# Zero matmuls, an earlier aT, an earlier x load and an earlier state transpose in a fused attention and maxout kernel

## The chip, the cores and the metric

The kernel runs on one core of one Trainium2 chip. The metric is the device time of one execution in microseconds (us). The engines are TensorE (PE; its weight loads are listed as PEld), VectorE (DVE), ScalarE (ACT), GpSimd (POOL) and SyncE (SP). Each engine works through its own instructions in the order in which the program gives them. DMAs are issued by SP, GpSimd and, once, ScalarE.

## The reference

Eight batches of cross attention between `x` (8 heads, 512 rows, 64 wide) and `state` (32 rows), read in both directions, followed by a feed-forward layer with a maximum of three products:

```python
scores = scale * x @ state.T            # per batch and head
xread  = softmax(scores) @ state        # 512 rows
sread  = softmax(scores.T) @ x          # 32 rows
tokens = concat([xread, sread])         # (8 * 544, 512) after merging heads
h      = max(max(tokens @ w1, tokens @ w2), tokens @ w3)   # 768 wide
out    = h @ w_out                      # (4352, 512) float32
```

## The kernel before

**Data.** Each batch's `x` is loaded as bfloat16 (`load_x`, a GpSimd DMA that converts). Half of batch 0 comes as float32 over SP and is converted by VectorE. The weights `w1`, `w2` and `w3` come in three chunks of two column blocks each (`load_w(0)` to `load_w(2)`, three GpSimd DMAs each), the states in four loads of two batches each (`load_st`). They are placed into `bd`, a block form of two heads side by side. For the first two pairs of batches the states are transposed on TensorE (`states`, line 127), for the last two by a DMA transpose on SP into `stT`, and then copied into `bd` by GpSimd (line 138, two copies for each pair).

**One batch.** `x_transpose` or `x_transpose_dma` makes `xT`. `scores` multiplies it with `bd` into `ps` and ScalarE writes the exponential `e`. `softmax` sums and inverts on VectorE (`den`, `rden`) and multiplies into `a` on GpSimd or VectorE (line 190). `a_transpose` (TensorE, then copies by ScalarE and VectorE, line 202) or `a_transpose_dma` (SP) makes `aT`. The state is not multiplied with `a` first: `g_cols` multiplies the state with the weights into `G` (line 248, copied out of PSUM at line 254), for six column blocks m of 128 columns. `x_maxout(b, m)` multiplies `G` with `aT` (line 269, six matmuls of 512 columns) for the three weights, and `maxout` takes their maximum: ScalarE copies the first (`t`, line 273), VectorE takes two maxima (lines 276 and 277) into `ht`. `ffn_out` multiplies `ht` with `wout` (line 306), ScalarE copies the result (line 309), and a DMA writes it out (line 318). `sread(b)` does the other direction; its result goes through a small SP DMA transpose (`late_transposes`) and is used at the very end (`s_maxout`).

**Order.** The order is written out by hand. Up to line 404 it is a straight list that starts batch 0, then interleaves batches 0, 1 and 2. `keep_busy(n)` issues n matmuls of zeros on TensorE. It stands three times in this list. From line 407 on a loop over batches b = 2 to 7 runs the six `x_maxout(b, m)`, and behind each of them a slot of further work: for the next batch n = b + 1 its scores (slot 0), softmax (slot 1) and DMA transposes (slot 2), and `ffn_out` of batch b - 1. In slot 2 the SP queue gets `a_transpose_dma(n)`, then `x_transpose_dma(n + 2)`, and, for n = 3 and n = 5, the states of batches 4 and 5, or 6 and 7. PSUM is used through two tags: "pw" with four buffers and "two" with two.

Of the kernel before, what the change touches and what calls it, by code (L numbers as in the profile page):

```python
# [15 lines left out]
def kernel(  # L16
# [16 lines left out]
    B, H, S, D = x.shape  # L33
# [20 lines left out]
    dve, act, pool = nc.vector.tensor_copy, nc.scalar.copy, nc.gpsimd.tensor_copy  # L54


    def load_st(k, eng):
        eng.dma_start(
            out=st_f[k],
            in_=state[2 * k:2 * k + 2].rearrange("b h n d -> (b h n) d").rearrange("(p t) d -> p t d", t=4))  # L60
# [8 lines left out]
    def load_x(b):  # L69
        nc.gpsimd.dma_start(  # L70
            out=x_sb[b][:, 0:XW].rearrange("p (h jd) -> p h jd", h=H),
            in_=x[b].rearrange("h (p j) d -> p h (j d)", j=J))
# [17 lines left out]
    def load_w(c):  # L90
        m0, m1 = chunks[c]
        for i, w in enumerate((moe_w1, moe_w2, moe_w3)):
            nc.gpsimd.dma_start(  # L93
                out=w_sb[c][:, :, i, :],
                in_=w.rearrange("(kk p) f -> p kk f", p=128)[:, :, m0 * 128:m1 * 128])

    def w_cols(m):
        c = [m0 <= m < m1 for m0, m1 in chunks].index(True)
        f = (m - chunks[c][0]) * 128
        return w_sb[c], slice(f, f + 128)  # L100
# [12 lines left out]
    def keep_busy(n):  # L113
        p = pp.tile([128, 1024], F32, tag="two", name="idle")
        for _ in range(n):
            nc.tensor.matmul(p[:, 0:512], zero[:, 0:128], zero, start=True, stop=True)  # L116


    def bd(b, h):
        return bds[b // 2][:, b % 2, h]  # L120
# [6 lines left out]
    def states(k, copy):  # L127

        if k < 2:
            p = pp.tile([128, 4, 128], BF16, tag="pw", bufs=4, name="pt")  # L130
            for t in range(4):
                nc.tensor.transpose(p[:, t, :], st[k][:, t].rearrange("p c d -> p (c d)"), ident)
        else:
            p = data.tile([128, 4, 128], BF16, name=f"stT{k}")
            nc.sync.dma_start_transpose(out=p, in_=st[k].rearrange("p t c d -> p (t c d)"))
        for c in range(2):
            r = slice(64 * c, 64 * c + 64)
            copy(out=bds[k][r, :, :, c, :].rearrange("p b h (q t) -> p (b h) q t", t=4),  # L138
                 in_=p[r].rearrange("p t (k q) -> p k q t", q=8))
# [4 lines left out]
    def new(d, b, shape, name, bufs=2):  # L144
        d[b] = work.tile(shape, BF16, tag=name, bufs=bufs, name=name)
# [13 lines left out]
    def x_transpose_dma(b):  # L159
        new(xT, b, [128, H, 2, 128], "xT", bufs=3)  # L160
        nc.sync.dma_start_transpose(out=xT[b].rearrange("p h j t -> p (h j) t"), in_=x_sb[b][:, 0:XW])  # L161
# [20 lines left out]
    def softmax(b, g0, g1, mul):  # L182
        n = g1 - g0
        if g0 == 0:
            new(a, b, [128, J, 2, HS, Ns], "a")
        den = work.tile([128, J, n, HS], F32, tag=f"den{n}", name="den")
        nc.vector.reduce_sum(out=den, in_=e[b][:, :, g0:g1], axis=AX.X)  # L187
        rden = work.tile([128, J, n, HS], F32, tag=f"rden{n}", name="rden")
        nc.vector.reciprocal(out=rden, in_=den)  # L189
        mul(  # L190
            out=a[b][:, :, g0:g1].rearrange("p j g s n -> p j (g s) n"),
            in0=e[b][:, :, g0:g1].rearrange("p j g s n -> p j (g s) n"),
            in1=rden.rearrange("p j g s -> p j (g s)").unsqueeze(3).to_broadcast((128, J, n * HS, Ns)))

    def a_transpose(b, g, copy):

        if g == 0:
            new(aT, b, [128, J, 2, 128], "aT", bufs=3)
        p = pp.tile([128, J, 128], BF16, tag="pw", bufs=4, name="pat")
        for j in range(J):  # L200
            nc.tensor.transpose(p[:, j, :], a[b][:, j, g].rearrange("p s n -> p (s n)"), ident)
        copy(out=aT[b][:, :, g, :], in_=p)  # L202

    def a_transpose_dma(b):
        new(aT, b, [128, J, 2, 128], "aT", bufs=3)
        nc.sync.dma_start_transpose(
            out=aT[b].rearrange("p j g t -> p (j g) t"), in_=a[b].rearrange("p j g s n -> p (j g s n)"))
# [26 lines left out]
    def flush_copies():  # L234
        while copies_due:
            copies_due.pop(0)()

    def g_cols(b, ms, copies=(nc.scalar.copy, nc.scalar.copy), defer=(False, False)):

        flush_copies()  # L240
        for m, copy, wait in zip(ms, copies, defer):
            if m == 0:
                new(G, b, [128, 2, NM * 384], "G", bufs=3)
            w, f = w_cols(m)
            p = pp.tile([128, 2, 512], F32, tag="two", name="pg")
            for s in range(HS):
                for g in range(2):
                    nc.tensor.matmul(  # L248
                        p[32 * s:32 * s + 32, g, 0:384].rearrange("p (i f) -> p i f", i=3),
                        bd(b, 2 * s + g)[64 * g:64 * g + 64, g, :], w[64 * g:64 * g + 64, s, :, f],  # L250
                        start=True, stop=True, tile_position=(64 * g, 32 * s))

            def place(m=m, p=p, copy=copy):
                copy(out=G[b][:, :, m * 384:(m + 1) * 384], in_=p[:, :, 0:384])  # L254

            if wait:
                copies_due.append(place)
            else:
                place()


    def maxout(b, m, n, lhs, rhs, nk):
        if m == 0:
            new(ht, b, [128, NM, n], "ht", bufs=4)
        pw = []
        for i in range(3):
            p = pp.tile([128, 512], F32, tag="pw", bufs=4, name=f"pw{i}")
            for k in range(nk):
                nc.tensor.matmul(p[:, 0:n], lhs(i, k), rhs(k), start=(k == 0), stop=(k == nk - 1))  # L269
            pw.append(p)  # L270
        t0 = work.tile([128, 512], BF16, tag="t0", name="t0")
        t1 = work.tile([128, 512], BF16, tag="t1", name="t1")
        nc.scalar.copy(out=t0[:, 0:n], in_=pw[0][:, 0:n])  # L273
        if copies_due:
            copies_due.pop(0)()
        nc.vector.tensor_max(t1[:, 0:n], t0[:, 0:n], pw[1][:, 0:n])  # L276
        nc.vector.tensor_max(ht[b][:, m, :], t1[:, 0:n], pw[2][:, 0:n])  # L277

    def x_maxout(b, m):
        maxout(b, m, 512,  # L280
               lambda i, k: G[b][:, k, m * 384 + i * 128:m * 384 + i * 128 + 128],
               lambda k: aT[b][:, :, k, :], 2)

    def s_maxout(m):
        w, f = w_cols(m)
        maxout("s", m, B * Ns, lambda i, k: w[:, k, i, f], lambda k: ats[:, :, k, :], HS)
# [51 lines left out]
    softmax(0, 0, 1, nc.gpsimd.tensor_mul)  # L338
    scores(0, 1, 2)
    softmax(0, 1, 2, nc.vector.tensor_mul)  # L340
    keep_busy(5)
    g_cols(0, (0,))
    a_transpose(0, 0, act)
    a_transpose(0, 1, dve)
    g_cols(0, (1,), (dve,))
    load_w(2)
    load_st(1, nc.gpsimd)
    x_maxout(0, 0)
    x_transpose(1, 0, act)
    x_transpose(1, 1, dve)  # L350
# [2 lines left out]
    scores(1, 1, 2)  # L353
    softmax(1, 0, 1, nc.gpsimd.tensor_mul)
    softmax(1, 1, 2, nc.gpsimd.tensor_mul)
    load_x(2)
    nc.gpsimd.dma_start(out=wout_sb, in_=moe_w_out.rearrange("(kk p) f -> p kk f", p=128))
    for k in range(2, B // 2):
        load_st(k, nc.gpsimd)
# [47 lines left out]
    for b in range(2, B):  # L407
        n = b + 1
        slots = [[] for _ in range(NM)]
        if n < B:  # L410
            slots[0].append(lambda: scores(n, 0, 2))
            slots[1].append(lambda: softmax(n, 0, 2, nc.gpsimd.tensor_mul))
            slots[2].append(lambda: a_transpose_dma(n))
            if n + 2 < B:
                slots[2].append(lambda: x_transpose_dma(n + 2))
            if n % 2 and n + 1 < B:
                slots[2].append(lambda: states((n + 1) // 2, pool))
            slots[5].append(late_transposes)
            if n + 3 < B:
                slots[0].append(lambda: load_x(n + 3))  # L420
        else:
            for m in range(NM):
                slots[m].append(lambda m=m: s_maxout(m))
        slots[1].append(lambda: g_cols(b, (2, 3)))
        slots[2].append(lambda: g_cols(b, (4, 5)))
        if n < B:
            slots[3].append(lambda: sread(n))
            slots[4].append(lambda: g_cols(n, (0, 1), defer=(False, True)))
        for j, m in enumerate((1, 2, 4, 5)):
            slots[m].insert(0 if m > 2 else len(slots[m]), lambda j=j: ffn_out(b - 1, j))  # L430
        for m in range(NM):
            x_maxout(b, m)
            for f in slots[m]:
                f()
# [36 lines left out]
```

## Time and profile before

| what | value |
|---|---|
| median of 11 runs | 165.45 us (160.22 to 169.97) |
| the profiled execution | 163.7 us, its span 161.9 us |
| mean granted TensorE clock | 0.984 |
| PE busy | 150.3 us (93%) |
| PEld busy | 71.2 us (44%) |
| DVE busy | 94.9 us (59%) |
| ACT busy | 96.6 us (60%) |
| POOL busy | 48.7 us (30%) |
| DMA moved | 21.72 MB, mean 134 GB/s |

The span runs from the first to the last instruction; the time of the execution is a little longer. The busy shares are averages over the whole span. The first third is a start in which TensorE waits for loads and for other engines, the rest a steady state in which TensorE is busy nearly without a break. A row of the timeline gives start, duration, engine, line, operation, output and input, and in brackets how long the engine stood idle before it and what ended this.

### The profile page before, as it was taken

The numbers are of one execution on the slowest core, as the hardware profiler recorded it, in microseconds if no ns is written. First come the engines' busy times: TensorE is split into PE (matmuls) and PEld (weight loads), VectorE is DVE, ScalarE is ACT, GpSimd is POOL, SyncE is SP. The second block draws the span as 40 slices with busy tenths as digits, with TensorE's granted clock in tenths as the row PEclk, the third lists the DMA queues.
The fourth block names the chain that finished last, engine by engine and source line by source line (L and its number), as shares of the span: only waits on it lengthen the run. The fifth ranks groups of instructions, "written<-read, shape, count | busy, mean of one in ns | idle before, by whom it ended". The sixth has DMA issues, their size and how long they took to land.

```text
span 161.9 us, 3570 instructions
## 1 busy us (share of the span) xinstructions
PE 150.3 (93%) x1433; PEld 71.2 (44%) x1433; DVE 94.9 (59%) x161; ACT 96.6 (60%) x156; POOL 48.7 (30%) x69
## 2 busy tenths in 40 slices
PE   7937979999999999899999997999999999999990
PEld 2413643454444444344444443444444475566450
DVE  4763796858536673577366735864667384475200
ACT  3224577799738827683888275837882837633340
POOL 8964069200733403641014034420141000100140
PEclk9996999999999999999999999999999999999997
DMA  3999949999799994597930965161307030030374
GB/s 127 189 180 196 197 86 105 162 232 186 119 195 196 234 183 93 194 191 197 144 130 0 122 117 203 60 163 42 134 0 202 0 136 0 0 134 0 130 223 166
DMA packets 35136, 21.72 MB, mean 134 GB/s; under 512 B 18832, under 2 KB 32784, under 8 KB 35120
## 3 DMA queue, kind: packets, MB, share of 16 engines
q0 software_dynamic: 15632, 15.08, 47.1%
q1 hardware_dynamic: 19344, 6.29, 21.2%
q8 instruction: 11, 0.18, 0.4%
q10 hardware_dynamic: 144, 0.13, 0.2%
q14 instruction: 5, 0.04, 0.1%
HBM read 15.20 MB, written 8.91 MB: 149 GB/s over the span
## 4 chain that ended last, share of the span: by engine, by line
PE 70%; DMA 7%; POOL 7%; issue 7%; ACT 3%; DVE 3%; SPq 1%; POOLq 0%; DVEq 0%
PE pw L269 36%; PE po L306 23%; PE pg L248 5%; DMA w<-in_moe_w_dram 5%; POOL bd L138 3%; POOL a L190 2%; PE psr L220 2%; PE ps L175 2%; ACT t L273 2%; DMA stT<-st 2%; DVE t L276 1%; SPq L161 1%; POOL w L93 1%; DVE ht L277 1%; PE ph L298 1%
## 5 line engine op out<-in xcount | busy, mean ns | idle before, releaser
L269 PE MATMUL pw<-aT,G 128*128 128x512 bf16 x288 | 71.2, 384 | 0.6 <-ACT aT L202 0.4
L276 DVE TENSOR_TENSOR t<-t,pw 128x512 bf16<-128x512 bf16 (+1 forms) x54 | 35.1, 651 | 43.3 <-ACT t L273 26.6
L306 PE MATMUL po<-wout,ht 128*128 128x512 bf16 x198 | 47.4, 380 | 0.0
L254 ACT CAST G<-pg 128x768 bf16<-128x768 f32 x46 | 35.7, 806 | 11.5 <-PE pg L248 11.1
L269 PEld LDWEIGHTS <-G 128*128 128x128 bf16 x288 | 26.7, 98 | 33.2 <-issue 4.9
L277 DVE TENSOR_TENSOR ht<-t,pw 128x512 bf16<-128x512 bf16 (+1 forms) x54 | 35.5, 658 | 5.6
L273 ACT CAST t<-pw 128x512 bf16<-128x512 f32 (+1 forms) x54 | 30.6, 566 | 13.5 <-PE pw L269 12.8
L309 ACT COPY osb<-po 128x512 f32<-128x512 f32 x33 | 19.3, 586 | 22.1 <-PE po L306 21.7
L306 PEld LDWEIGHTS <-ht 128*128 128x128 bf16 x198 | 17.8, 98 | 24.1 <-issue 4.0
L190 POOL TENSOR_TENSOR a<-e,rden 128x1024 bf16<-128x1024 bf16 (+1 forms) x9 | 14.5, 1618 | 43.4 <-DVE rden L189 33.1
L318 POOL DMA_DIRECT2D out_dram<-osb x14 | 8.0, 570 | 45.2 <-ACT osb L309 36.6
L248 PE MATMUL pg<-w,bd 64*32 64x384 bf16 x384 | 13.0, 331 | 3.5 <-DMA w<-in_moe_w_dram 2.9
L187 DVE TENSOR_REDUCE den<-e 128x32 f32<-128x1024 bf16 (+1 forms) x10 | 9.9, 991 | 0.8 <-ACT e L180 0.8
L180 ACT ACTIVATE e<-ps 128x1024 bf16<-128x1024 f32 x6 | 6.1, 1024 | 5.7 <-PE ps L175 5.6
L248 PEld LDWEIGHTS <-bd 64*32 64x32 bf16 x384 | 3.6, 89 | 12.5 <-issue 11.6
L269 PE MATMUL pw<-ats,w 128*128 128x256 bf16 x72 | 8.8, 273 | 0.0
L138 POOL COPY bd<-stT 64x512 bf16<-64x512 bf16 x4 | 4.2, 1056 | 14.4 <-DMA stT<-st 14.3
L269 PEld LDWEIGHTS <-w 128*128 128x128 bf16 x72 | 7.0, 98 | 2.1
L116 PE MATMUL idle<-zero 128*128 128x512 bf16 x15 | 5.9, 547 | 1.2 <-DVE zero L81 1.2
L93 POOL DMA_DIRECT2D w<-in_moe_w_dram x9 | 6.8, 771 | 0.0
L175 PEld LDWEIGHTS <-xT 128*128 128x128 bf16 x128 | 4.8, 98 | 4.4 <-issue 2.1
L70 POOL DMA_DIRECT2D x<-in_x_dram x7 | 6.5, 932 | 0.0
(46 smaller groups left out, 67.7 us busy)
## 6 DMA issues: line engine op xcount, KB each, us to landing
out_dram<-osb POOLq DMA_DIRECT2D x14, 512.0 KB, 3.5
x<-in_x_dram POOLq DMA_DIRECT2D x7, 512.0 KB, 10.0
w<-in_moe_w_dram POOLq DMA_DIRECT2D x9, 256.0 KB, 10.2
wout<-in_moe_w_out_dram POOLq DMA_DIRECT2D x1, 768.0 KB, 10.3
x0f<-in_x_dram SPq DMA_DIRECT2D x1, 512.0 KB, 3.9
out_dram<-osb SPq DMA_DIRECT2D x1, 512.0 KB, 2.7
stf<-in_state_dram POOLq DMA_DIRECT2D x3, 128.0 KB, 9.9
x<-in_x_dram POOLq DMA_DIRECT2D x1, 256.0 KB, 4.8
```

The lines of the kernel that those rows point to most:

```text
L93: nc.gpsimd.dma_start(out=w_sb[c][:, :, i, :], in_=w.rearrange("(kk p) f -> p kk f", p=128)[:, :, m0 * 128:m1 * 128])
L138: copy(out=bds[k][r, :, :, c, :].rearrange("p b h (q t) -> p (b h) q t", t=4), in_=p[r].rearrange("p t (k q) -> p k q t", q=8))
L187: nc.vector.reduce_sum(out=den, in_=e[b][:, :, g0:g1], axis=AX.X)
L190: mul(out=a[b][:, :, g0:g1].rearrange("p j g s n -> p j (g s) n"), in0=e[b][:, :, g0:g1].rearrange("p j g s n -> p j (g s) n"), in1=rden.r ...
L248: nc.tensor.matmul(p[32 * s:32 * s + 32, g, 0:384].rearrange("p (i f) -> p i f", i=3), bd(b, 2 * s + g)[64 * g:64 * g + 64, g, :], w[64 * ...
L254: copy(out=G[b][:, :, m * 384:(m + 1) * 384], in_=p[:, :, 0:384])
L269: nc.tensor.matmul(p[:, 0:n], lhs(i, k), rhs(k), start=(k == 0), stop=(k == nk - 1))
L273: nc.scalar.copy(out=t0[:, 0:n], in_=pw[0][:, 0:n])
L276: nc.vector.tensor_max(t1[:, 0:n], t0[:, 0:n], pw[1][:, 0:n])
L277: nc.vector.tensor_max(ht[b][:, m, :], t1[:, 0:n], pw[2][:, 0:n])
L306: nc.tensor.matmul(p, ht[b][:, m, j * 128:(j + 1) * 128], wout_sb[:, m, :], start=(m == 0), stop=(m == NM - 1))
L309: act(out=o[:, j, :], in_=p)
```

## The change

Four places in the order change; no operation's size or engine does.

1. The third `keep_busy` issues nine zero matmuls instead of five.
2. The transposes of `a` of batch 0 come ahead of column block 0 of its `G`; on ScalarE and VectorE the copies of `aT` come ahead of those of `G`.
3. `load_x(2)` moves, on GpSimd, from behind the softmax multiplications of batch 1 to a place ahead of them, directly behind the third chunk of W and the second load of states.
4. In slot 2 of the loop, for n = 3 and n = 5, the transpose of the states comes ahead of that of `x` on SP.

```diff
     softmax(0, 1, 2, nc.vector.tensor_mul)
-    keep_busy(5)
-    g_cols(0, (0,))
+    keep_busy(9)
     a_transpose(0, 0, act)
     a_transpose(0, 1, dve)
+    g_cols(0, (0,))
     g_cols(0, (1,), (dve,))
     load_w(2)
     load_st(1, nc.gpsimd)
+    load_x(2)
     x_maxout(0, 0)
...
     softmax(1, 0, 1, nc.gpsimd.tensor_mul)
     softmax(1, 1, 2, nc.gpsimd.tensor_mul)
-    load_x(2)
     nc.gpsimd.dma_start(out=wout_sb, in_=moe_w_out.rearrange("(kk p) f -> p kk f", p=128))
...
             slots[2].append(lambda: a_transpose_dma(n))
+            if n % 2 and n + 1 < B:
+                slots[2].append(lambda: states((n + 1) // 2, pool))
             if n + 2 < B:
                 slots[2].append(lambda: x_transpose_dma(n + 2))
-            if n % 2 and n + 1 < B:
-                slots[2].append(lambda: states((n + 1) // 2, pool))
```

## The prediction

> **What bounds the kernel.** I read the page's chain first, then the waits by engine, then the timeline of the first 28 us, then PE's rows with an idle time in the rest. In the chain TensorE is nearly everything:
>
> ```profile
> PE 70%; DMA 7%; POOL 7%; issue 7%; ACT 3%; DVE 3%; SPq 1%; POOLq 0%; DVEq 0%
> PE pw L269 36%; PE po L306 23%; PE pg L248 5%; DMA w<-in_moe_w_dram 5%; POOL bd L138 3%; POOL a L190 2%; PE psr L220 2%; PE ps L175 2%; ACT t L273 2%; DMA stT<-st 2%; DVE t L276 1%; SPq L161 1%; POOL w L93 1%; DVE ht L277 1%; PE ph L298 1%
> ```
>
> PE is busy 150.3 of 161.9 us. So only what PE waits for, or works off at a low clock, can be won. The list of waits names the places that the change touches:
>
> ```profile
> POOL bd L138 <- DMA stT<-st: 14.3, 2, 7.2
> ...
> PE pg L248 <- DMA w<-in_moe_w_dram: 2.9, 1, 2.9
> ...
> PE ps L175 <- POOL bd L138: 1.6, 2, 0.9
> ```
>
> The columns are total, count, longest. The 14.3 us are GpSimd's own and cost nothing by themselves. PE's 1.6 us come from the two late states. PE's 2.9 us are the wait for the first W chunk, which no edit shortens. What follows it can be shortened (timeline from 12 to 18 us; start, duration):
>
> ```profile
> 12.70 0.36 PE L248 MATMUL pg<-w,bd 64*32 64x384 bf16 x8 [2.89 <-DMA w<-in_moe_w_dram]
> ...
> 12.99 0.65 PE L201 MATMUL pat<-ident,a 128*128 128x128 bf16 x8
> 13.13 0.80 ACT L254 CAST G<-pg 128x768 bf16<-128x768 f32 x1 [3.76 <-PE pg L248]
> ...
> 13.82 0.59 ACT L202 COPY aT<-pat 128x512 bf16<-128x512 bf16 x1
> ...
> 14.46 2.62 PE L269 MATMUL pw<-aT,G 128*128 128x512 bf16 x6 [0.37 <-ACT aT L202]
> ...
> 17.82 1.46 PE L269 MATMUL pw<-aT,G 128*128 128x512 bf16 x6
> ```
>
> ScalarE copies G (0.80), then aT (0.59), and only then does the first maxout start. The same six matmuls take 2.62 us at 14.46 and 1.46 us at 17.82. The table by windows, cut at the points where the granted clock turns (13.45 and 16.86), says why; PE's busy time stands first after the length, PEclk third from the end:
>
> ```profile
> 6.61:10.03 3.42, 2.67 (x34) 1.54 (x32) 2.48 (x5) 1.19 (x2) 1.86 (x4) 1.00 1.34 175
> 10.03:13.44 3.41, 0.74 (x16) 0.59 (x16) 1.43 (x3) 0.31 (x1) 3.41 (x5) 1.00 1.39 184
> 13.44:16.85 3.41, 3.04 (x18) 1.06 (x15) 1.79 (x3) 1.56 (x3) 0.35 (x1) 0.50 1.45 196
> ```
>
> A stretch of 3.41 us with 0.74 us of PE work is followed by one of the same length at half clock.
>
> **Part 1: start of batch 0.** Four zero matmuls more: the five now spread over 1.24 us from 8.57, about 0.216 apart, so nine end near 10.7. GpSimd's a of head half 0 is done at 10.99, VectorE's of half 1 at 11.53. The zero matmuls thus lie in PE's idle time; the cover is 0.3 us, and each 0.216 us beyond it would delay the transposes, which themselves have cover: they are 8 matmuls in two groups of about 0.4 us, done near 12.0, while the first W chunk lands at 12.57 (its last piece is issued at 3.86 and lands 8.71 us later). The order adds one wait ahead of G: PE's transposes wait for a at 11.53, and behind them stand both G columns, then the maxout; with 0.6 us to spare until W it costs nothing. ScalarE (0.59) and VectorE (0.42) copy aT by about 12.6, in idle time. Then G: matmuls at 12.70, copy 13.13 to 13.93, maxout at 13.97 instead of 14.46: **0.49 us** gained.
>
> The clock: in the stretch 10.03 to 13.44 there will be 0.6 us of zero matmuls, 0.8 of transposes and 0.75 of G, 2.1 us (62%) instead of 0.74 (22%). The trace shows 22% followed by half clock and 2.67 (78%) by full clock; what decides between is not shown. The bounds are a gain of 0 and of 2.62 - 1.46 = 1.16 us. The Trainium skill, "TensorE: Matmul & The Clock Gate", section "Part 4: PE-mode transpose", speaks against the change: transposes don't count as busy PE for the gate in the same way. By it only 0.6 + 0.75 = 1.35 us (40%) count, nearer to the row that dropped; by the plain busy row 62%, nearer to the one that held. The rule cannot be tested on the row of before, since 0.45 us of its 0.74 are transposes and it drops either way. I take full clock, as 62% is nearest to 78%, with the other end kept as a rival. The first maxout then ends 0.49 + 1.16 = 1.65 us earlier.
>
> **What is late next.** x of batch 1 lands at 4.59 + 10.6 = 15.2, and its transposes would start at about 15.3: just in. Scores of batch 1 go from 19.11 to 17.45. But behind them on PE stand the G columns 2 and 3, at 19.68 now. The three W pieces of that chunk, by the DMA view, are issued at 6.12, 6.87 and 7.62 and land 10.5, 11.0 and 11.6 us later: 16.6, 17.9 and **19.2**. PE will wait there for 1.1 us, and G column 2 is earlier by 0.43 only. From there I step on: ScalarE, free of the exponentials by then, copies it 19.67 to 20.47 (now 20.52 to 21.33); G column 0 of batch 1 goes 20.5 instead of 21.38; its ScalarE copy ends near 21.7, t of maxout (0,2) near 22.3, VectorE's t and ht near 23.8 instead of 24.96. a of batch 1 is ready near 22.1 instead of 23.75, so the transposes no longer stop PE (0.27 us). What the stage hands on is earlier by 24.96 - 23.8, **1.1 us**; full 1.65 were W in time; 0.45 with the clock at half, since then only the 0.49 remain and W hides a little.
>
> **Part 2: x of batch 2.** Its one GpSimd DMA issue of 0.95 us moves from 23.69 to about 13.8, ahead of the two multiplications of batch 1. GpSimd stands idle there for 7.90 us, until 21.69 (20.0 after part 1), so the issue is hidden; without that cover it would cost 0.95 us before a. In the queue it is ahead of wout, states 2 and 3, x3 and x4, and all of these issue 0.95 us earlier. Nobody waits for them on PE now: x2 lands at 23.69 + 6.4 = 30.1 and is transposed at 32.98; wout lands at 34.9, first used at 37.89. So the sum gets **0**. It comes behind the third W chunk, which lands at 23.3 and is used at 35.7.
>
> **Part 3: states ahead of x.** Twice (batches 4 and 6), SP issues aT, xT, stT; afterwards aT, stT, xT.
>
> ```profile
> 56.17 1.25 SPq L206 DMA_TRANSPOSE aT<-a  x1
> 57.59 3.08 SPq L161 DMA_TRANSPOSE xT<-x  x1
> 60.73 1.26 SPq L135 DMA_TRANSPOSE stT<-st  x1
> ```
>
> stT starts 3.1 us earlier and lands 2.5 us after its start, or, if it has to follow aT (which lands at 60.2), at 61.4 at the latest; the two GpSimd copies take 2.18 us, done by 63.6. PE's scores are ready for them at 64.76:
>
> ```profile
> 65.47 0.63 PE L175 MATMUL ps<-bd,xT 128*128 128x64 bf16 x16 [0.71 <-POOL bd L138]
> 98.00 0.63 PE L175 MATMUL ps<-bd,xT 128*128 128x64 bf16 x16 [0.86 <-POOL bd L138]
> ```
>
> Both waits go, **0.71 + 0.86 = 1.57 us**; the second place has the same intervals (aT at 88.63, scores wanted at 97.14). The price is one stT issue, 1.26 to 1.51 us, ahead of xT of batches 5 and 7 and the sread transpose behind them on SP. xT of batch 5 now lands at 62.0 and is read at 81.22; the delay would have to be over 15 us. Behind the copies on GpSimd stand two output DMAs, which become free earlier. From 98 to 156 us no PE row shows idle time, so what is won is kept to the end.
>
> **Sum.** 1.1 + 0 + 1.57 = 2.7 us. Against the profiled execution, 163.7 (span 161.9 and 1.8 around it), that is 161.0. The median shown is 165.45; I take the same microseconds from it: **162.7 us**, -1.6%. The 11 runs spread from 160.22 to 169.97, so a measurement of this kernel tells about 2%, 3.3 us, from no change, and the forecast lies just inside.
>
> **Rivals and chances.**
> - **Forecast, 0.45:** 162.7, own range 161.2 to 164.2. By the spread, two fifths of this case fall over 2%.
> - **More is won, 0.27:** W's second chunk is not the limit, or most runs hold more of these waits than the profiled one. For: the median is 1.75 us above the profiled execution, and something is longer there. Against: the pieces land evenly, 1.3 us apart, by the queue's pace. Full 1.65 + 1.57 = 3.2 gives 162.2; with the 1.75 as well 160.5. Nearly all of it counts as faster.
> - **Less is won, 0.17:** the clock drops all the same, 0.45 + 1.57 = 2.0, 163.4 us; or stT is held by other transfers and its 1.57 stays, 164.3. Against the latter: stT lands 2.5 and 2.7 us after its issue even behind xT.
> - **Slower, 0.11: x2 takes W's place.** At 13.8 us the second W chunk is still in transit. If packets of x2 are served between its own, its landing moves by up to x2's transfer time: 512 KB against 256 KB per 1.33 us, 2.66 us, so 19.2 becomes 21.9. Then G column 2 is 2.2 us later than now, and less the 1.57 of part 3 the kernel is 0.6 us slower: 166.1. It decides once the chunk lands after 19.68 + 1.57 = 21.25. For: the queue holds many transfers at once (landing takes 10 us). Against: the third chunk, queued from 10.9 on, lands after the second, at 20.5, 21.9 and 23.3, in the order of issue.
>
> Faster: 0.45 x 0.4 + 0.27 = 0.45. Slower by over 2% needs 3.3 us, more than this mechanism gives; with other slow causes I keep 0.10. Within 2%: 0.45. The range goes from 160.2 (all won and the spread) to 165.4 (nothing won).
>
> **What would show it.** Right: the first maxout starts near 14.0 and takes about 1.46 us at PEclk 1.00; PE waits for a W transfer at about 18.1 to 19.2; no PE row waits for POOL bd; x2 lands near 26. Wrong: PEclk 0.50 over 3.4 us about 14 to 17; the second W chunk landing after 20; L175 still behind L138, or behind xT; a new PE wait for ScalarE or VectorE between 24 and 35 that takes back the first stage's gain.

## The result, and the profile after

The changed kernel is faster by about 1%: the ratio of its times to those of before is **0.9905, with a 95% interval of 0.9863 to 0.9947**. On the 163.7 us of the profiled execution that is 1.6 us less (0.9 to 2.2), where 2.7 were forecast. The medians of all executions, 160.2 us (12) and 163.93 us (47), lie further apart: the ratio leaves out those more than 1.5% above the fastest of their kernel, 4 of the 12 and 32 of the 47, and as no experiment shows what makes these long, it is the number to use.

The profile of after is one of the four, with 165.2 us and a span of 163.4. Its start can be compared, and its middle shows what a late transpose does. First the start, rows of the timeline from 10 to 19 us (start, duration, engine, line, operation, and in brackets the idle time before and what ended it):

```profile
10.92 0.40 PE L201 MATMUL pat<-ident,a 128*128 128x128 bf16 x4 [0.36 <-POOL a L190]
11.47 0.40 PE L201 MATMUL pat<-ident,a 128*128 128x128 bf16 x4 [0.15 <-DVE a L190]
...
11.79 0.52 PE L248 MATMUL pg<-w,bd 64*32 64x384 bf16 x16
...
12.22 0.80 ACT L254 CAST G<-pg 128x768 bf16<-128x768 f32 x1 [0.28 <-PE pg L248]
...
13.08 1.47 PE L269 MATMUL pw<-aT,G 128*128 128x512 bf16 x6 [0.76 <-ACT G L254]
...
18.32 0.52 PE L248 MATMUL pg<-w,bd 64*32 64x384 bf16 x16 [0.96 <-DMA w<-in_moe_w_dram]
```

Every forecast step is there. aT is out of the way before G, the maxout starts as soon as ScalarE has copied G, and it takes 1.47 us instead of 2.62. Then TensorE waits 0.96 us for the second W chunk. The clock held, in the table by windows (PE's busy time first after the length, granted clock third from the end):

```profile
10.03:13.44 3.41, 2.14 (x29) 0.84 (x28) 2.69 (x5) 1.38 (x2) 3.41 (x5) 1.00 1.38 184
13.44:16.85 3.41, 3.41 (x33) 1.98 (x31) 2.26 (x4) 2.08 (x3) 1.11 (x2) 1.00 1.45 196
```

TensorE is busy for 2.14 us (63%) where it was busy for 0.74. But note the row at 11.79: no wait for W stands in its bracket. In this execution the first chunk landed near 11.5, not at 12.57, and G waited for the transposes of a.

Now SP's rows and the scores' rows in the middle:

```profile
45.14 5.29 SPq L161 DMA_TRANSPOSE xT<-x  x1
54.22 1.24 SPq L206 DMA_TRANSPOSE aT<-a  x1
55.51 2.57 SPq L135 DMA_TRANSPOSE stT<-st  x1
58.25 4.31 SPq L161 DMA_TRANSPOSE xT<-x  x1
```

```profile
62.57 1.46 PE L269 MATMUL pw<-aT,G 128*128 128x512 bf16 x6 [1.06 <-DMA aT<-a]
66.55 0.63 PE L175 MATMUL ps<-bd,xT 128*128 128x64 bf16 x16 [2.52 <-POOL bd L138]
```

stT does stand ahead of xT now, as forecast. But xT of batch 4, issued at 45.14, was in transit for 13.6 us in this execution, until 58.7. aT took 8.2 us to land behind it (4.0 before) and stT 8.8 (2.5 before), and TensorE waited for both, 1.06 and 2.52 us. For what the states' new place does when xT lands sooner, this profile is the wrong one; the experiment with the states alone shows it.

### The profile page after: what moved, and what is told of

Its sections match the earlier page's. It is cut to its first block, busy times and chain, and to the rows that moved or that the text cites. A ratio compares the mean times of both kernels' runs of the same rounds, so it can differ in the third digit from the quotient of the medians.

```text
span 163.4 us, 3578 instructions
## 1 busy us (share of the span) xinstructions
PE 151.5 (93%) x1437; PEld 71.2 (44%) x1437; DVE 95.1 (58%) x161; ACT 96.8 (59%) x156; POOL 48.7 (30%) x69
## 4 chain that ended last, share of the span: by engine, by line
PE 72%; DMA 12%; POOL 7%; DVE 3%; ACT 1%; issue 1%; SPq 1%; POOLq 0%; DVEq 0%
PE pw L269 37%; PE po L306 24%; DMA w<-in_moe_w_dram 6%; PE pg L248 6%; DMA stT<-st 5%; POOL w L93 2%; PE psr L220 2%; PE ps L175 2%; DVE t L276 2%; POOL bd L138 1%; POOL a L190 1%; DVE ht L277 1%; PE ph L298 1%; SPq L206 1%; ACT t L273 1%
## 5 line engine op out<-in xcount | busy, mean ns | idle before, releaser
L306 PE MATMUL po<-wout,ht 128*128 128x512 bf16 x198 | 48.2, 384 | 0.0
L116 PE MATMUL idle<-zero 128*128 128x512 bf16 x19 | 6.8, 512 | 1.2 <-DVE zero L81 1.2
```

What stands on the lines that cost most here:

```text
L306: nc.tensor.matmul(p, ht[b][:, m, j * 128:(j + 1) * 128], wout_sb[:, m, :], start=(m == 0), stop=(m == NM - 1))
```

## The experiments

**Part by part.** The first three kernels do one part of the change each, the fourth does all but the move of x.

`start_only` (items 1 and 2 in the list of changes, part 1 of the prediction):

```diff
-    keep_busy(5)
-    g_cols(0, (0,))
+    keep_busy(9)
     a_transpose(0, 0, act)
     a_transpose(0, 1, dve)
+    g_cols(0, (0,))
```

> Only the start changes: nine zero matmuls and aT of batch 0 ahead of its G; x of batch 2 and the states stay as before. Theory A (the sizes of the prediction hold): 1.1 us less, ratio 0.993; the first maxout starts 0.5 us after the first W chunk's G copy order is relieved and takes 1.46 us at full clock, and PE then waits about 1 us for the second W chunk; both waits for the block form of the states (0.7 and 0.9 us) remain. Theory B (nearly all of the gain of 1.5 us is the start, since the waits for the states vanish only in the profiled execution): 1.5 us less, ratio 0.991. Theory C (the clock of before drops only in some executions, so the start is worth only its 0.5 us): ratio 0.997.

Measured: **0.9996 (0.9967 to 1.0025)**. Nothing is won, within 0.5 us. Theory A and theory B fall for the start, and even C's 0.5 us lies at the edge.

`x2_only` moves `load_x(2)` behind `load_st(1)`, ahead of the multiplications.

> Only the load of x of batch 2 moves ahead of the multiplications. Theory A and B: nobody waits for it, ratio 1.000. Rival D (x2 takes transfer time from the second W chunk): that chunk lands after 20 us, up to 2.2 us more, ratio up to 1.013. Rival E (the earlier load thins out the transfers later, when SP's transposes and the loads of x collide): the waits for the states get shorter and the ratio falls below 0.997.

Measured: **1.0008 (0.9965 to 1.0052)**, from seven of its 22 executions. The second W chunk's last piece landed 10.9 us after its issue (11.6 in the profile of before), so D has nothing to stand on. Nor has E: the two waits for the block form are still there, 1.14 and 0.84 us.

`states_only` puts `states` ahead of `x_transpose_dma` in slot 2.

> Only the states' transposes go ahead of x's. Theory A: both PE waits for the block form (0.71 and 0.86 us) are gone, 1.57 us less, ratio 0.990. Theory B (stT is held by the transposes that are still in flight, whatever stands ahead of it, or the waits exist only in the profiled execution): 0 to 0.3 us, ratio 0.998 to 1.000. Theory C: at least 1.0 us less, ratio 0.994 or lower.

Measured: **0.9866 (0.9830 to 0.9902)**, 2.2 us (1.6 to 2.8). This part alone brings all that the change brings. The rows of the scores in its profile, and then those of `start_only`, which keeps the old order of the states:

```profile
47.05 0.63 PE L175 MATMUL ps<-bd,xT 128*128 128x64 bf16 x16
62.81 0.63 PE L175 MATMUL ps<-bd,xT 128*128 128x64 bf16 x16
78.57 0.63 PE L175 MATMUL ps<-bd,xT 128*128 128x64 bf16 x16
94.33 0.63 PE L175 MATMUL ps<-bd,xT 128*128 128x64 bf16 x16
```

```profile
46.85 0.63 PE L175 MATMUL ps<-bd,xT 128*128 128x64 bf16 x16
63.09 0.63 PE L175 MATMUL ps<-bd,xT 128*128 128x64 bf16 x16 [0.32 <-POOL bd L138]
78.84 0.63 PE L175 MATMUL ps<-bd,xT 128*128 128x64 bf16 x16
96.01 0.63 PE L175 MATMUL ps<-bd,xT 128*128 128x64 bf16 x16 [1.25 <-POOL bd L138]
```

These rows are the cleanest measure of the steady state: without a wait, one batch takes 15.76 us from scores to scores. With the old order the two batches that need stT take 16.24 and 17.17, 0.48 and 1.41 too many, **1.89 us** together. In the profile of before the rows ahead of the two in the prediction are

```profile
48.84 0.63 PE L175 MATMUL ps<-bd,xT 128*128 128x64 bf16 x16
81.22 0.63 PE L175 MATMUL ps<-bd,xT 128*128 128x64 bf16 x16
```

so the two batches take 65.47 - 48.84 = 16.63 and 98.00 - 81.22 = 16.78, also 1.89 us too many. That the two sums agree is chance: in the other profiles with the old order and no late xT they are 2.0 (`w_short`), 2.3 (`x2_only`), 2.8 (`w_short_start`) and 2.9 us (`zeros_only`). With stT ahead of xT, in `states_only`, all batches take 15.76. And this is how stT comes in:

```profile
54.40 1.25 SPq L206 DMA_TRANSPOSE aT<-a  x1
55.69 1.37 SPq L135 DMA_TRANSPOSE stT<-st  x1
57.24 1.32 SPq L161 DMA_TRANSPOSE xT<-x  x1
59.06 2.20 POOL L138 COPY bd<-stT 64x512 bf16<-64x512 bf16 x2 [4.69 <-DMA stT<-st]
```

stT lands 3.3 us after 55.69, GpSimd's copies run from 59.06 to 61.26, and the scores at 62.81 find them done with 1.5 us to spare.

`start_and_states` is the whole change without the move of x.

> The whole change without the move of x of batch 2. Theory A: 2.7 us less by the sum, ratio 0.983, the same as the whole change; B: the same as the whole change, 0.990; C: 0.990. Rival D (x2's earlier load costs): better than the whole change by 0.5 us or more. Rival E (it helps later): worse than the whole change by 0.5 us or more.

Measured: **0.9895 (0.9858 to 0.9932)**, the same as the whole change within the intervals. The three parts multiplied, 0.9996 x 1.0008 x 0.9866, give 0.987; whether the missing 0.3% is more than spread the intervals don't tell.

**Why is the start worth nothing?** Its gain was seen in a trace, and it is gone in the time. Two kernels split it.

`zeros_only` has only `keep_busy(9)` instead of `keep_busy(5)`.

> Only the four zero matmuls more; G stays ahead of aT. Theory H (the start brings nothing on the whole because the granted clock drops in only a part of the executions of before and the new order makes G wait for a when W lands early): the clock never drops at the start, so no execution with a mean granted clock near 0.986 is left, and the early G is kept; 0.1 to 0.4 us less, ratio 0.997 to 1.000. Theory I (the clock is what the start is worth): ratio 0.993.

Measured: **0.9983 (0.9944 to 1.0021)**, which is against theory I.

`order_only` has only the new order of aT and G, with five zero matmuls.

> Only aT of batch 0 ahead of its G; five zero matmuls as before, so that TensorE does nothing but 0.8 us of transposes between about 9.7 us and the landing of W. If transposes hold the clock as other matmuls do, nearly no execution shows the mean clock of 0.984 to 0.990 that a drop at the start gives, which a third or more of the executions of before show; if they do not count, as many show it as before. Time: theory H 0.0 to 0.3 us less, ratio 0.998 to 1.000; theory I, with transposes not counting, 1.000.

Measured: **1.0051 (1.0005 to 1.0098)**, a little slower, which no theory had; why is not shown.

The mean granted clock of every execution behind the ratios says how often the clock drops at the start. A drop there gives a mean of 0.984 to 0.989 (one elsewhere would count too).

| kernel | executions compared | of these with a mean clock below 0.99 |
|---|---|---|
| before, in the three sets | 33, 19, 25 | 9, 6, 6 |
| order_only | 10 | 5 |
| zeros_only | 13 | 0 |
| start_only | 16 | 0 |
| start_and_states | 12 | 0 |
| states_only, x2_only, w_short, states_sread, states_early (five zero matmuls) | 29 | 4 |
| after, w_short_start, start_states_sread (nine) | 27 | 0 |
| start_early_sread (nine) | 11 | 3 |

So the profile of before, with its drop, shows what happens in only 21 of the 77 executions, and with 163.7 us it is longer than any of them. In the first set those with the drop average 162.2 us, the others 161.7: it costs some 0.6 us there, and 0.8 to 1.1 in the other two sets. A quarter of that is 0.2 us, which is what `zeros_only` shows and what the interval can't tell from nothing. With four more zero matmuls the drops at the start end; the three in `start_early_sread` can lie elsewhere, since TensorE has waits of 1.15 and 1.71 us there at 61 and 78 us (below). The new order alone doesn't end them, with 0.8 us of transposes in the same gap.

Why the order doesn't pay shows in the profiles side by side. All times are us; W is the landing of the last piece of the first W chunk, and "hand-over" is the row of line 269 near 32 us that ends with a wait for VectorE's ht, which every kernel passes. The last column is worked out before rounding.

| kernel | W | first G matmul | first maxout | clock dropped | wait for the 2nd W chunk | hand-over | hand-over less W |
|---|---|---|---|---|---|---|---|
| before | 12.6 | 12.70 | 14.46 | yes | none | 34.28 | 21.7 |
| x2_only | 11.9 | 12.02 | 13.78 | yes | none | 33.36 | 21.5 |
| states_only | 11.7 | 11.84 | 13.60 | no | 0.64 | 32.50 | 20.8 |
| zeros_only | 10.7 | 10.87 | 12.63 | no | 0.65 | 31.55 | 20.8 |
| order_only | 12.0 | 12.13 | 13.41 | no | 1.11 | 32.81 | 20.8 |
| start_only | 11.5 | 11.69 | 12.97 | no | 1.04 | 32.30 | 20.8 |
| after | 11.5 | 11.79 | 13.08 | no | 0.96 | 32.33 | 20.8 |
| start_and_states | 10.3 | 12.09 | 13.37 | no | none | 32.04 | 21.7 |

Three things stand in it. With W late enough, the new order brings the first maxout 1.28 us after the first G matmul instead of 1.76, 0.48 us as forecast. But where the clock has not dropped and TensorE waits for the second W chunk, the hand-over comes 20.8 us after W with the old order and with the new one: the half microsecond goes into a longer wait for that chunk. From the end of this wait to the hand-over it is 14.00 or 14.01 us in all five profiles, so there the chunk's landing sets the time, whatever came before. In `start_only`, with the new order:

```profile
18.29 0.52 PE L248 MATMUL pg<-w,bd 64*32 64x384 bf16 x16 [1.04 <-DMA w<-in_moe_w_dram]
32.30 1.46 PE L269 MATMUL pw<-aT,G 128*128 128x512 bf16 x6 [0.19 <-DVE ht L277]
```

And where W lands early, at 10.3 us, the new order makes G wait for a until 12.09, and the whole advance of W is lost. The rows of `zeros_only`, with the old order, show the other side of it:

```profile
10.87 0.35 PE L248 MATMUL pg<-w,bd 64*32 64x384 bf16 x8 [0.42 <-DMA w<-in_moe_w_dram]
11.16 0.62 PE L201 MATMUL pat<-ident,a 128*128 128x128 bf16 x8
...
12.63 1.45 PE L269 MATMUL pw<-aT,G 128*128 128x512 bf16 x6 [0.57 <-ACT aT L202]
...
17.55 0.52 PE L248 MATMUL pg<-w,bd 64*32 64x384 bf16 x16 [0.65 <-DMA w<-in_moe_w_dram]
...
31.55 1.46 PE L269 MATMUL pw<-aT,G 128*128 128x512 bf16 x6 [0.18 <-DVE ht L277]
```

With W at 10.7 the maxout starts at 12.63. In the profiles with the new order it starts at 12.97 at the earliest, since VectorE finishes a at 11.30 there (`start_only`) and the transposes of a come next.

**Is it the second W chunk?** Two kernels leave out one third of that chunk and have zeros in its place.

```diff
         for i, w in enumerate((moe_w1, moe_w2, moe_w3)):
+            if c == 1 and i == 2:
+                nc.gpsimd.memset(w_sb[c][:, :, i, :], 0.0)
+                continue
```

`w_short` has the old start:

> The kernel before, but the third piece of the second W chunk (w3, column blocks 2 and 3) is not loaded; zeros are written there instead, so that this chunk lands some 1.3 us sooner. Theory F (the gain of the start is lost at the wait for this chunk): the unchanged start gains little from it, 0 to 0.6 us, ratio 0.996 to 1.000, since it reaches that place at about 17.9 us and the chunk landed at 18.4 to 19.2. Theory G (the start's gain is lost elsewhere): no change, 1.000.

Measured: 0.9919 (0.9873 to 0.9965), 1.3 us less, more than F forecast and against G's none. `w_short_start` has the new one:

> As the last one, with nine zero matmuls and aT of batch 0 ahead of its G. Theory F: no wait for the second W chunk after the scores of batch 1, which now start near 17.0; the start is worth 0.5 us where the clock was full before and 1.1 to 1.6 us where it had dropped, so 0.5 to 1.0 us under the last kernel, 0.993 to 0.996 of before. Theory G: equal to the last kernel within 0.2 us.

Measured: 0.9988 (0.9944 to 1.0032). Against theory F, the new start is not faster in time; by these ratios it is slower, though the intervals just overlap. In the profiles it is faster: the wait for the chunk is gone from both, and hand-over less W is 31.44 - 10.9 = 20.5 with the old start and 32.08 - 12.0 = 20.1 with the new one, 0.4 us less. But W itself landed 1.1 us apart in these two executions, more than the effect. So that the start's half microsecond goes into the wait for the second chunk is read from the rows; this pair of kernels, meant to show it in the time, doesn't, and where the 1.3 us of `w_short` come from is open.

**Filling that wait.** `states_sread` is `states_only`, and `start_states_sread` is `start_and_states`, with work that needs no W moved ahead of it:

```diff
+    sread(0)
     g_cols(0, (2, 3), (act, dve))
-    sread(0)
```

> The states' transposes ahead of x's, and sread of batch 0 (0.56 us of TensorE work that needs no W) ahead of the G columns 2 and 3, where TensorE waits for W. Theory F: with the old start the wait of about 0.6 us is filled, 0.3 to 0.5 us less than the states alone, ratio 0.984; the granted clock still drops at the start in some executions. Theory G: as the states alone, 0.987.

Measured: 0.9844 (0.9786 to 0.9903).

> The last one with nine zero matmuls and aT ahead of G as well. Theory F: the wait for W, about 1.0 us with the new start, is filled for 0.56 us; 0.4 to 0.6 us less than start and states without it, ratio 0.984 to 0.986, and about equal to the last kernel, since the chunk's landing sets the time in both. Theory G: 0.988 to 0.990, as without the move.

Measured: 0.9851 (0.9796 to 0.9907). Both are in the expected place, and neither can be told from its twin without the move (0.9866 and 0.9895). In the profile of `start_states_sread` the wait for W is 0.53 us instead of about 1.0 in the other profiles with the new order, and the next one, for ScalarE's copy of G, grows from 0.19 to 0.76: most of the wait has only changed its name. From the chunk's G to the hand-over it is 13.84 us, 0.16 less than 14.00.

**States still earlier.** `states_early`:

```diff
+    states(2, pool)
     late_transposes()
     x_transpose_dma(4)
...
+            if n == 3:
+                slots[2].append(lambda: states(3, pool))
             if n + 2 < B:
                 slots[2].append(lambda: x_transpose_dma(n + 2))
-            if n % 2 and n + 1 < B:
-                slots[2].append(lambda: states((n + 1) // 2, pool))
```

> The states' transposes still earlier: of batches 4 and 5 ahead of the loop (ahead of xT of batch 4), of batches 6 and 7 in the slot of n = 3. Theory A (the waits for the block form are worth 1.9 us and are gone once stT stands ahead of xT): the same as the states alone, 0.987; nothing is left to gain in an undisturbed execution. The long wait that the profile of the changed kernel shows at 64 us (xT of batch 4 in transit for 13.6 us, aT and stT behind it) can't hit the states any more. Rival (stT ahead of xT still waits for aT and the block form is close to late): 0.984 or lower.

Measured: 0.9862 (0.9757 to 0.9967), from two of its six executions and too wide to rank. Its profile speaks against it: TensorE waits 1.94 and 0.93 us for aT of batches 3 and 4, where `states_only` has no such wait. `start_early_sread` adds the rest of the change and the move of sread:

> The changed kernel with the states still earlier as in the last one, and sread of batch 0 ahead of the G columns 2 and 3. Theory H with A: the states' 1.9 us and half of the wait for the second W chunk, ratio 0.984 to 0.987; at least as fast as the changed kernel (0.9905), by 0.3 to 0.6 us.

Measured: **1.0060 (1.0018 to 1.0101)**, slower than before and against the expectation. Its profile has no wait for the block form left, but two others:

```profile
62.53 1.46 PE L269 MATMUL pw<-aT,G 128*128 128x512 bf16 x6 [1.15 <-DMA aT<-a]
80.16 1.46 PE L269 MATMUL pw<-aT,G 128*128 128x512 bf16 x6 [1.71 <-DMA aT<-a]
```

```profile
52.30 2.20 POOL L138 COPY bd<-stT 64x512 bf16<-64x512 bf16 x2 [5.20 <-DMA stT<-st]
54.44 0.89 POOL L70 DMA_DIRECT2D x<-in_x_dram  x1
55.40 1.91 POOL L190 TENSOR_TENSOR a<-e,rden 128x1024 bf16<-128x1024 bf16 x1
```

GpSimd waits 5.20 us for stT in the wrong place. Behind it stand the load of x of batch 6 (54.44, where `states_only` has 47.40) and the multiplication that makes a (55.40 instead of 52.46). aT of batch 3 is issued at 57.33 instead of 54.40 and lands late; aT of batch 4 takes 8.8 us to land instead of 5.4. GpSimd's rows in `states_early` are the same in kind (a wait of 4.32 us for stT, that load at 52.83, that multiplication at 53.78). That the later loads cause aT of batch 4 to land late was not tried by itself.

## Why the prediction was right and wrong

The sign and the range held: the ratio makes 163.9 us of the median of 165.45, inside 161.2 to 164.2. That is in part luck: the range was wide enough for the loss of a whole term. The sum of 2.7 us against a measured 1.6 (0.9 to 2.2) had one term that was worth nothing and one that was a little too small.

- **The start, 1.1 us, measured 0.06 (-0.4 to 0.5): the step that failed.** It took one profiled execution as the rule. "With 0.6 us to spare until W it costs nothing" was read from a landing of 12.57, the latest in these profiles; W lands between 10.3 and 12.6, and with an early W the transposes of a have no cover and hold G up. The 1.16 us for the clock were real in that execution, but it drops in 21 of 77.
- **What is late next** was named rightly: the second W chunk, with a wait of 1.1 us forecast and 0.96 to 1.11 seen. The forecast still let 1.1 us of the start's gain pass it, because in that execution the old start, with its clock dropped, came to the chunk after its landing. An undropped old start already waits there (0.64 us), and then nothing passes.
- **The clock.** 62% busy was forecast, 63% seen, and full clock came of it. The weighed rule of the Trainium skill, that transposes don't count for the gate ("TensorE: Matmul & The Clock Gate", "Part 4: PE-mode transpose"), fits `order_only`, with a drop in 5 of 10, against none in 13 with the zeros alone. It isn't shown by it: counting the transposes as busy, the emptiest 3.41 us at the start of the profile of `order_only` (9.60 to 13.01) hold 1.31 us of TensorE's work, 38%, about as little as was followed by half clock elsewhere (37%, in the last section).
- **x of batch 2, 0 us:** right, 1.0008, as far as the seven executions behind that ratio show. It lands at 25.3, near the 26 forecast. The rival in which it takes W's place is out. One wait was overlooked: its issue was held until x of batch 1 had landed (below). GpSimd's idle time hid that too.
- **The states, 1.57 us, measured 2.2 (1.6 to 2.8), and 1.89 in the rows.** The mechanism was right in each step. The brackets that gave 0.71 and 0.86 count idle time from the modelled end of the matmul before; from scores to scores the loss was 0.87 and 1.02. The other profiles with the old order, 1.9 to 2.9 us, cover the measured 2.2.

Of the versions run, the states alone (0.9866), with or without the move of sread, is at least as good as the whole change (0.9905). The intervals overlap, so it isn't shown to be better.

## What to carry to other kernels

A stall read from one profile of a start that waits for DMA is one draw: before pricing its removal, ask what the row would be if the load landed a microsecond sooner, and what then has to wait for what the change moved ahead of it. A wait in a steady state, which comes back in each profile, can be priced, and best from period to period of the same row rather than from the idle time in a bracket. And moving a DMA earlier also moves what its receiver blocks: the consumer's queue has to be checked as well as the issuer's.

## What the hardware showed that was not expected

- The clock's stretches have no fixed place, but a fixed length. In the profile of before it dropped at 13.45 and came back at 16.86, in that of `x2_only` at 12.3 and 15.7, in that of after, behind the wait of 2.52 us, at 67.9 and 71.2: each time some 3.4 us at half clock. The gaps that led to them, 2.89, 2.39 and 2.52 us, were shorter than that. A gap of 1.26 us, in `states_only`, brought none. In all four profiles with such a stretch ahead of the last microseconds, the full clock had lasted a whole number of 3.41 us until then, counted from where it began: 2 in before and `x2_only`, 18 in after, 19 in `order_only`. Cut in this way, the 3.41 us just ahead of the half clock hold 22%, 30%, 37% and 0% of TensorE's work, and the emptiest that were followed by full clock 43% (`order_only` from 62.58, `states_early` from 59.27). The full clock began at 4.3 to 7.2 us, differently in each profile. So whether one gap falls into one such piece or is shared by two differs from execution to execution, which would be a reason why the same kernel drops in some only; this was not tried by itself.
- A GpSimd DMA can wait for a much earlier one. The thirteenth, x of batch 2 in its new place, was held until the fifth, x of batch 1, had landed:

```profile
14.45 0.89 POOL L70 DMA_DIRECT2D x<-in_x_dram  x1 [0.79 <-DMA x<-in_x_dram]
```

  In the traces of before, after and `x2_only` GpSimd's DMAs from the ninth to the sixteenth each wait for the semaphore that the one eight issues earlier sets. In `x2_only` the issue of x was held for 1.27 us.
- The same transpose can take very different times to land: aT of batch 3, 3.9 us in `states_only` and 8.2 us in the profile of after, behind an xT that was in transit for 13.6 (10.2 in `states_only`).
